# Batches 0 and 1 of an attention and MLP kernel: from pairs of heads with keys in chunks of 112 to quads of heads with keys in chunks of 64

## The chip, the core and the metric

The kernel runs on one core of a Trainium2 chip. The metric is the device time of one execution in microseconds, taken as the median over several runs. TensorE (PE), VectorE (DVE), ScalarE (ACT), GpSimd (POOL) and the sync engine (SP) each work through their own queue of instructions in order and wait for each other with semaphores.

## The reference

```python
def _attn_ref(q, k, v):            # 8 batches, 12 heads, 448 tokens, 64 per head
    scale = 1.0 / np.sqrt(q.shape[-1])
    scores = scale * np.matmul(q, k.transpose(0, 1, 3, 2))
    m = np.max(scores, axis=-1, keepdims=True)
    e = np.exp(scores - m)
    attn = e / (np.sum(e, axis=-1, keepdims=True) + np.exp(-m) + 1e-09)
    return np.matmul(attn, v)

def _moe_ref(x, w_in, w_out):      # x: 3584 x 768, w_in: 768 x 2048, w_out: 2048 x 768
    h = x @ w_in
    r = np.maximum(h, 0.0)
    return (r * r) @ w_out
```

The twelve heads of a token, side by side, are the row x of the second part. All inputs and the output are float32 in HBM. Since e is divided by its sum plus exp(-m), the maximum cancels, and the kernel computes exp(scores) / (sum + 1) without it.

## The kernel before

All matrix work is in float16. An order written out by hand sets what each engine does when; there is no scheduler behind it. Batch by batch, the attention of one batch is interleaved with the projections of the batches before it, so that TensorE always has something to stream.

**Attention.** Scores are computed transposed, keys on partitions and queries in columns. Queries and keys are first "flipped" on TensorE (transposed against an identity into PSUM, lines L191 and L211, then copied to the tile `qk`, L193 and L217). `exp` (L222) goes from the PSUM tile `sp`, of which there are two buffers, to the tile `et`. Row sums come from a matmul against a block of ones, which spreads the sum over 64 partitions; Ln with a bias and Exp with scale -1 on ACT turn it into the reciprocal `rcp` (L290 and L291, in quads L378 and L379). The values are a matmul of v against `et` (L273, in quads L390), and one multiplication on VectorE (L299, L302, L396) writes the normalised result to `xt`, the input of the projections.

**Two ways to tile it.** Batches 2 to 7 work in quads of four heads with keys in chunks of 64 (`visit`, L332 and L346; `values_quad`; `sums_quad`): a score or value matmul uses a 64x64 quarter of the array, and four run side by side. A quad is seven chunks, and one exponential covers 128 partitions by 896 elements. Batches 0 and 1 work in pairs of two heads with keys in chunks of 112 (P), four chunks for a pair: a score matmul uses 64 rows by 112 columns of the array (L241), a value matmul 112 rows by 64 columns (L273), and two run side by side. VectorE adds the exponentials of the four chunks first (`add_chunks`: L257 and L260 in batch 0, L253 and L255 in batch 1), so that the row sums are one matmul a head (L287).

**Stages.** Batch 0's queries come in two parts, the first 192 (FIRST) and then 256, each for six pairs; `units` lists them. While the first part runs TensorE has no projection work; `keep_warm` puts matmuls on zeros in between. From then on `tile_in` (L419: x times w_in, then ReLU and square on VectorE, L431 and L433, into `gs`) is handed out in pieces by `drain`, whose shares are written out for each unit. `tiles_in_early` starts two such tiles with the pairs that are ready. In mode COLS2 a projection matmul uses 128 rows by 64 columns of the array, two side by side. Batch 1 follows in six units of all 448 queries, with the rest of batch 0's input projection, and with the flips of batch 2's first two quads. Its last pair is finished inside the loop of batch 2.

From there a loop over the batches begins. `between` issues twelve or eleven visits of quads, with output projection tiles (`tile_out`, L491 in mode SQUARE, 64x64 quarters of the array) and values between them by a count of planned time; then eight input projection tiles run (`run(ins, ...)`), a second `between`, and eight more. `second` hands out the output tiles, in the order first and second half of the 768 columns; each half needs the matching half of `wout`.

**Loads.** q and k of the first three pairs come as float32 on the queues of SP and ACT (L119), one transfer of 224 KB each, into buffers of the exponentials' pool, and are cast by `cast` (L201 on ACT, L203 on VectorE). All else comes by GpSimd's queue, cast to float16 on the way, in this order: v, q and k of the other pairs (L108, L126), `win` in eight pieces (L132) with batch 1's first q and k in their middle, the rest of batch 1, then batch 2's q and k (L99) and `wout` (L136), which are issued after the last unit of batch 0, then batch 2's last quad, its v (L91) and the staged copies for batch 3 (L155). A load into a buffer that is in use waits, and holds up what GpSimd has queued behind it.

Of the kernel before, what the change touches and what calls it, by code (L numbers as in the profile page):

```python
# [16 lines left out]
def kernel(  # L17
# [9 lines left out]
    nc = tc.nc  # L27
# [4 lines left out]
    NPAIR = H // 2  # L32
# [3 lines left out]
    P = S // RUN  # L36
    NQ = H // 4
    KC = S // 64
    PAIRED = (0, 1)
# [15 lines left out]
    e_pool = ctx.enter_context(tc.tile_pool(name="e", bufs=4))  # L55
# [17 lines left out]
    q_r = q.rearrange("b h (p t) d -> b p h t d", t=RUN)  # L73
    k_r = k.rearrange("b h (p t) d -> b p h t d", t=RUN)
    v_r = v.rearrange("b h (p t) d -> b p h t d", t=RUN)
# [3 lines left out]
    whole, vns, qks, xts, naturals, stages = {}, {}, {}, {}, {}, {}  # L79
# [5 lines left out]
    def load_v_quads(b):  # L85
        vn = vns[b] = v_pool.tile([128, NQ, 2, KC, D], FP16, name="vn")
        for i in range(2):
            rows_ = vn[64 * i:64 * i + 64].rearrange("p g j c d -> p (g j) (c d)")
            parts = ((0, KC),) if b in ON_PE else ((0, KC - 1), (KC - 1, KC))
            for c0, c1 in parts:  # L90
                nc.gpsimd.dma_start(out=rows_[:, :, c0 * D:c1 * D], in_=quads_of(v, 64 * c0, 64, c1 - c0)[b, i])  # L91

    def load_natural_quads(b, g0, g1):
        t = nat.tile([128, RUN * 2 * S], FP16, name=f"nn{0 if g0 == 0 else 1}")
        w = 2 * S
        for n, r in enumerate((q, k)):
            part = t[:, n * (g1 - g0) * w:(n + 1) * (g1 - g0) * w].rearrange("p (h x) -> p h x", x=S)
            for i in range(2):
                nc.gpsimd.dma_start(out=part[64 * i:64 * i + 64], in_=quads_of(r, 0, 64, KC)[b, i][:, 2 * g0:2 * g1])  # L99
            for g in range(g0, g1):  # L100
                naturals["qk"[n], b, "quad", g] = part[:, 2 * (g - g0):2 * (g - g0) + 2].rearrange(
                    "p j (c d) -> p j c d", d=D)

    def load_v(b, p0, p1):
        hs = slice(2 * p0, 2 * p1)
        if b not in vns:
            vns[b] = v_pool.tile([P, H, RUN, D], FP16, name="vn")
        nc.gpsimd.dma_start(out=vns[b][:, hs], in_=v_r[b, :, hs])  # L108

    def load_natural(b, p0, p1):  # L110

        raw = b == 0 and p1 <= 3
        for n, r in (("q", q_r), ("k", k_r)):
            src = r[b, :, 2 * p0:2 * p1]
            if raw:
                if p0 == 0:
                    whole[n] = e_pool.tile([P, RUN * S], FP32, name="et")
                t = whole[n][:, p0 * 512:(p0 + 1) * 512].rearrange("p (h t d) -> p h t d", h=2, t=RUN)
                (nc.sync if n == "q" else nc.scalar).dma_start(out=t, in_=src)  # L119
            else:  # L120
                if p0 % 3 == 0 and n == "q":
                    whole["both"] = nat.tile([P, RUN * 2 * S], FP16, name=f"nn{p0 // 3}")
                w = NPAIR * RUN * D
                t = whole["both"][:, w * (n == "k"):w * (n == "k") + w].rearrange("p (h t d) -> p h t d", t=RUN, d=D)
                t = t[:, 2 * (p0 % 3):2 * (p0 % 3 + p1 - p0)]
                nc.gpsimd.dma_start(out=t, in_=src)  # L126
            for pr in range(p0, p1):
                naturals[n, b, pr] = t[:, 2 * (pr - p0):2 * (pr - p0) + 2]
# [55 lines left out]
    def transposes_quad(b, g):  # L184
        if b not in qks:
            qks[b] = qk_pool.tile([128, 3, COLS], FP16, name="qk")
        for n in range(2):
            tp = mp_tile(FP16).rearrange("p a x -> p (a x)")
            for c in range(KC):
                for j in range(2):  # L190
                    nc.tensor.transpose(tp[64 * j:64 * j + 64, 128 * c:128 * c + 128],  # L191
                                        naturals["qk"[n], b, "quad", g][:, j, c, :], ident)
            nc.vector.tensor_copy(  # L193
                qks[b][:, n, 2 * S * g:2 * S * (g + 1)].rearrange("p (i c x) -> p c i x", i=2, c=KC),
                tp[:, 0:2 * S].rearrange("p (c i x) -> p c i x", c=KC, i=2))

    def cast(b, pr):
        for name in "qk":
            f = flat.tile([P, 2, RUN, D], FP16, name=f"flat{name}")
            if pr < 2 and name == "k":  # L200
                nc.scalar.activation(out=f, in_=naturals[name, b, pr], func=AF.Copy)  # L201
            else:
                nc.vector.tensor_copy(f, naturals[name, b, pr])  # L203
            naturals[name, b, pr] = f

    def transposes(b, pr):
        tp = mp_tile(FP16)
        for i, name in enumerate("qk"):
            for s in range(RUN):
                for h in range(2):  # L210
                    nc.tensor.transpose(tp[64 * h:64 * h + 64, i, P * s:P * s + P],  # L211
                                        naturals[name, b, pr][:, h, s, :], ident[0:P, 0:P])
# [641 lines left out]
```

## Time and profile before

| | us |
|---|---|
| median of 3 runs | 407.98 (407.74 to 408.20) |
| the profiled execution | 407.64 |
| its span | 405.9 |
| TensorE busy | 394.9 (97%) |
| VectorE busy | 277.2 (68%) |
| ScalarE busy | 224.1 (55%) |
| GpSimd busy | 59.5 (15%) |
| L222, all exponentials to `et`, 132 instructions | 118.0 |
| L419, all input projection matmuls to `mp`, 1248 instructions | 109.0 |
| moved by DMA | 45.83 MB |

The profile is of one execution. Its span goes from the first to the last instruction on the core; the time of the execution has 1.7 us around it. Busy time of an engine counts each moment once, but the busy times of groups on TensorE overlap, since several matmuls run side by side, and can't be added. A timeline line gives start, length, engine, line of the kernel, operation, the tile written, the tiles read, the shape and the count; in brackets stands the time that the engine was idle before it and what ended the wait. PE is matmul and PEld the load of its stationary operand.

### The profile page before, as it was taken

The page shows a single profiled execution, that of the slowest core. Times are in us where ns is not written, and L with a number is a line of the kernel's source. Part 1 is how long each engine was busy: PE and PEld are TensorE (multiplying, and loading weights), DVE is VectorE, ACT ScalarE, POOL GpSimd, SP SyncE. Part 2 cuts the span into 40 slices and gives each one's busy share as a digit, 9 for nine tenths or more (in the row PEclk, how much of TensorE's full clock was granted, in tenths as well). Part 3 has the DMA queues.
Part 4 walks back from the last instruction along what each step waited for, and adds up shares of the span by engine and source line. Part 5 has one row for each costly group of instructions (what it writes and reads, how often), then busy time and mean ns, then how long its engine had stood idle before and what let it go on. Part 6 is the DMA issues. An engine that isn't in the chain of part 4 may idle for free.

```text
span 405.9 us, 14479 instructions
## 1 busy us (share of the span) xinstructions
PE 394.9 (97%) x6627; PEld 262.4 (65%) x6627; DVE 277.2 (68%) x507; ACT 224.1 (55%) x277; POOL 59.5 (15%) x93
## 2 busy tenths in 40 slices
PE   7899998999999999999999999999999999999997
PEld 3567676667676666757666675757666675555664
DVE  3778888786967867686967867686967868186000
ACT  4898986928465564836466473836466473100111
POOL 6524140005000320003200440005000000000000
PEclk9999999999999999999999999999999999999999
DMA  9999999498706794186925694186501020100222
GB/s 186 197 197 198 203 204 208 105 196 113 175 3 126 122 186 102 42 134 144 189 69 129 119 191 95 42 155 122 120 3 40 3 80 4 48 31 0 79 78 79
DMA packets 77118, 45.83 MB, mean 113 GB/s; under 512 B 46720, under 2 KB 71552, under 8 KB 77056
## 3 DMA queue, kind: packets, MB, share of 16 engines
q0 software_dynamic: 30128, 22.16, 36.5%
q1 hardware_dynamic: 46208, 22.05, 24.5%
q8 instruction: 52, 0.85, 0.9%
q10 hardware_dynamic: 720, 0.69, 0.7%
q14 instruction: 10, 0.08, 0.1%
HBM read 45.69 MB, written 17.93 MB: 157 GB/s over the span
## 4 chain that ended last, share of the span: by engine, by line
PE 87%; DVE 5%; ACT 3%; DMA 2%; issue 1%; ACTq 0%; DVEq 0%
PE mp L491 26%; PE mp L419 22%; PE mp L421 10%; PE xp L419 6%; PE mp L390 6%; PE sp L346 5%; PE xp L421 4%; ACT et L222 2%; DMA et<-in_k_dram 2%; PE sp L241 2%; PE xp L273 2%; PE sp L332 1%; PE mp L211 1%; PE xp L491 1%; PE sp L375 1%
## 5 line engine op out<-in xcount | busy, mean ns | idle before, releaser
L222 ACT ACTIVATE et<-sp 128x896 f16<-128x896 f32 (+3 forms) x132 | 118.0, 915 | 26.0 <-PE sp L346 13.0
L491 PE MATMUL mp<-wout,gs 64*64 64x384 f16 x1760 | 125.6, 323 | 0.0
L419 PEld LDWEIGHTS <-win 128*64 128x64 f16 x1536 | 85.0, 110 | 47.7 <-issue 7.2
L419 PE MATMUL mp<-xt,win 128*64 128x448 f16 (+2 forms) x1248 | 109.0, 324 | 2.2 <-DVE qk L193 1.3
L491 PEld LDWEIGHTS <-gs 64*64 64x64 f16 x2624 | 76.2, 107 | 23.0 <-issue 0.6
L491 PE MATMUL xp<-wout,gs 64*64 64x384 f16 x864 | 84.7, 323 | 0.0
L431 DVE TENSOR_SCALAR rt<-mp 128x448 f16<-128x448 f32 (+2 forms) x82 | 51.0, 622 | 19.0 <-PE mp L419 8.4
L433 DVE TENSOR_TENSOR gs<-rt 128x448 f16<-128x448 f16 (+2 forms) x128 | 50.4, 395 | 12.0 <-ACT rt L429 7.9
L222 ACT ACTIVATE nn<-sp 128x896 f16<-128x896 f32 x42 | 37.6, 913 | 14.0 <-PE sp L346 12.3
L429 ACT ACTIVATE rt<-mp 128x448 f16<-128x448 f32 x18 | 9.8, 543 | 60.0 <-PE mp L419 48.3
L498 DVE TENSOR_SCALAR ot<-mp 128x384 f32<-128x384 f32 x41 | 22.7, 554 | 27.3 <-PE xp L491 19.9
L181 POOL COPY flatq<-qk 64x384 f16<-64x384 f16 x20 | 13.6, 704 | 186.9 <-DMA qk<-stage_k 186.6
L421 PEld LDWEIGHTS <-gs 128*128 128x128 f16 x256 | 24.4, 98 | 15.1 <-issue 0.4
L346 PE MATMUL sp<-qk 64*64 64x224 f16 x720 | 32.9, 258 | 0.0
L419 PE MATMUL xp<-xt,win 128*64 128x448 f16 x288 | 31.3, 352 | 0.0
L421 PE MATMUL mp<-wout,gs 128*128 128x384 f16 (+2 forms) x192 | 29.6, 313 | 0.0
L346 PEld LDWEIGHTS <-qk 64*64 64x64 f16 x720 | 22.4, 119 | 10.7 <-issue 3.6
L500 ACT ACTIVATE ot<-mp 128x384 f32<-128x384 f32 (+2 forms) x12 | 5.6, 463 | 42.4 <-PE mp L421 42.4
L396 DVE TENSOR_TENSOR xt<-mp,rcp 128x448 f16<-128x448 f32 x34 | 19.7, 619 | 8.2 <-PE mp L390 7.8
L378 ACT ACTIVATE rcp<-sp,one_b 128x896 f32<-128x896 f32 x18 | 18.1, 1003 | 6.3 <-PE sp L371 6.3
L390 PEld LDWEIGHTS <-vn 64*64 64x64 f16 x504 | 14.4, 107 | 6.1 <-issue 0.4
L390 PE MATMUL mp<-et,vn 64*64 64x448 f16 x308 | 18.3, 349 | 0.0
(82 smaller groups left out, 392.6 us busy)
## 6 DMA issues: line engine op xcount, KB each, us to landing
out_dram<-ot SPq DMA_DIRECT2D x9, 384.0 KB, 2.3
win<-in_moe_w_in_dram POOLq DMA_DIRECT2D x8, 384.0 KB, 14.0
wout<-in_moe_w_out_dram POOLq DMA_DIRECT2D x4, 768.0 KB, 17.8
vn<-in_v_dram POOLq DMA_DIRECT2D x10, 288.0 KB, 5.4
out_dram<-ot SPq DMA_DIRECT2D x15, 192.0 KB, 3.0
stage_q<-in_q_dram POOLq DMA_DIRECT2D x4, 676.0 KB, 9.8
stage_k<-in_k_dram POOLq DMA_DIRECT2D x4, 676.0 KB, 12.3
out_dram<-ot SPq DMA_DIRECT2D x7, 288.0 KB, 6.0
```

What stands on the lines that cost most here:

```text
L181: nc.gpsimd.tensor_copy(km[rows_].rearrange("p h (x o) -> p h x o", o=2)[:, :, :, odd], src[:, :, S // 2 - 32:S // 2])
L222: nc.scalar.activation(out=out_, in_=in_, func=AF.Exp, scale=scale)
L346: nc.tensor.matmul(sp[64 * i:64 * i + 64, o, j * n:(j + 1) * n], keys, qk[r, 0, h * n:(h + 1) * n], start=True, stop=True)
L378: nc.scalar.activation(out=rcp, in_=zp[:, :, 0:S], func=AF.Ln, bias=one_b)
L390: nc.tensor.matmul(xps[i][64 * j:64 * j + 64, 0:S], vns[b][r, g, j, c, :], of_column(e[r], m, j), start=(c == 0), stop=(c == KC - 1))
L396: nc.vector.tensor_mul(xts[b][:, NQ * i + g, :], xps[i][:, 0:S], zqs[m][:, i, :])
L419: nc.tensor.matmul(out_[x:x + 64], lhsT[:, x:x + 64], rhs, start=start, stop=stop)
L421: nc.tensor.matmul(out_, lhsT, rhs, start=start, stop=stop)
L431: nc.vector.tensor_scalar(out=rt[:, 0:m], in0=hp[:, 0:m], scalar1=0.0, scalar2=None, op0=ALU.max)
L433: nc.vector.tensor_mul(gs[:, f0:f0 + per, t0 % RING:t0 % RING + n], r, r)
L491: nc.tensor.matmul(o[y:y + 64, 0:w], g[x:x + 64, y:y + 64], wout[x:x + 64, fb, n0:n0 + w], start=(fb == 0), stop=(fb == NFFB - 1))
L498: nc.vector.tensor_scalar(out=ot[:, n0:n0 + w], in0=op[:, 0:w], scalar1=OUT_SCALE, scalar2=None, op0=ALU.mult)
```

## The change

Batches 0 and 1 take the form of the others. The code of the pairs goes (`scores`, `add_chunks`, `values`, `row_sums`, `normalise`, `tiles_in_early`, `drain` and the list of units), and with it `keep_warm` but for the nine matmuls at the very start. Batch 0 keeps its two parts of 192 and 256 queries. Each part has three quads, and each quad four visits: two chunks of 64 keys in one exponential, and one chunk in the last. Its sums are no longer added on VectorE: all seven chunks accumulate on TensorE (`part_sums`), in a buffer of the scores' pool. Batch 1 uses `visit` and `values_quad`; VectorE adds six of its chunks to two, and `sums_quad` accumulates these two and the seventh chunk on TensorE. Sums and values of a quad are issued among the visits of the next one, and those of batch 1's last quad inside the loop of batch 2. Projection tiles are issued whole (`fill`) at written-out places. Inside a projection tile the order of the heads is such that the last quad comes last.

The first loads come by quad and by chunk: queries 0 to 2 (chunks of 64) and keys 0 to 2 of quad 0, keys 3 to 6, then queries 0 to 2 and all keys of quad 1; what is left of the queries of batch 0 comes later in one piece by GpSimd. `wout` is loaded in two halves, the second behind batch 2's last quad and v. The exponentials' pool has five buffers instead of four. Flips and their copies to `qk` are issued in pieces that follow the loads, and two pieces may share one PSUM tile. Batches 0 and 1 are stored in rows of seven tokens instead of four.

```diff
-    e_pool = ctx.enter_context(tc.tile_pool(name="e", bufs=4))
+    e_pool = ctx.enter_context(tc.tile_pool(name="e", bufs=5))
...
+    def transposes(b, g, *groups):
+        if b not in qks:
+            qks[b] = qk_pool.tile([128, 3, COLS], FP16, name="qk")
+        for pieces in groups:
+            tp = mp_tile(FP16).rearrange("p a x -> p (a x)")
+            o = 0
+            for n, c0, c1, copy in pieces:
+                flips(tp, o, b, g, n, c0, c1)
+                flipped(copy, tp, o, b, g, n, c0, c1)
+                o += 128 * (c1 - c0)
...
+    def part_visit(p, g, v):
+        q0, n = ((0, FIRST), (FIRST, S - FIRST))[p]
+        e = part_e(p, g)
+        cs = range(2 * v, min(2 * v + 2, KC))
+        sp = s_psum.tile([128, 2, 512], FP32, name="sp")
+        for c in cs:
+            for i in range(2):
+                for j in range(2):
+                    r = slice(64 * j, 64 * j + 64)
+                    x = (2 * g + i) * S
+                    o = (c - cs[0]) * n
+                    nc.tensor.matmul(sp[64 * i:64 * i + 64, j, o:o + n], qks[0][r, 1, x + 64 * c:x + 64 * c + 64],
+                                     qks[0][r, 0, x + q0:x + q0 + n], start=True, stop=True)
+        exp(e[:, cs[0]:cs[-1] + 1].rearrange("p c j n -> p j c n"),
+            sp[:, :, 0:len(cs) * n].rearrange("p j (c n) -> p j c n", n=n))
+
+    def part_sums(p, g):
+        n = (FIRST, S - FIRST)[p]
+        e = part_e(p, g)
+        zp = s_psum.tile([128, 2, 512], FP32, name="sp")
+        for c in range(KC):
+            for i in range(2):
+                for j in range(2):
+                    r = slice(64 * i, 64 * i + 64)
+                    nc.tensor.matmul(zp[64 * j:64 * j + 64, i, 0:n], ones[r], e[r, c, j], start=(c == 0),
+                                     stop=(c == KC - 1))
+        parts[p, g, "z"] = reciprocals(zp, n)
...
     def sums_quad(m, in_cols):
-        es = esq.pop(m)[:, 0:2 * S]
+        es = esq.pop(m)
+        sums = [es[:, 0:2 * S]]
+        if QUADS[m][0] == 1:
+            sums += [es[:, 2 * S:4 * S], chunk_quad(m, KC - 1)]
...
-    for pr in range(3):
-        load_natural(0, pr, pr + 1)
+    for g in range(2):
+        raw = e_pool.tile([128, RUN * S], FP32, name="et")
+        load_chunks(nc.sync, heads(raw, 0, 2, 3), 0, 0, g, g + 1, 0, 3)
+        if g == 0:
+            load_chunks(nc.scalar, heads(raw, 384, 2, 3), 1, 0, g, g + 1, 0, 3)
+            load_chunks(nc.sync, heads(raw, 768, 2, 4), 1, 0, g, g + 1, 3, KC)
+        else:
+            load_chunks(nc.scalar, heads(raw, 384, 2, KC), 1, 0, g, g + 1, 0, KC)
...
     keep_warm(9)
-    cast(0, 0)
-    transposes(0, 0)
-    keep_warm(1)
-    cast(0, 1)
...
+    cast(0, (0, 0, 3, nc.vector), (1, 0, 3, nc.scalar), (1, 3, KC, nc.vector))
+    transposes(0, 0, [(0, 0, 3, on_dve), (1, 0, 3, on_act)])
+    part_visit(0, 0, 0)
+    transposes(0, 0, [(1, 3, KC, on_dve)])
+    part_visit(0, 0, 1)
+    cast(1, (0, 0, 3, nc.vector), (1, 0, KC, nc.vector))
+    transposes(0, 1, [(0, 0, 3, on_dve), (1, 0, 3, on_dve)], [(1, 3, KC, on_dve)])
+    part_visit(0, 0, 2)
+    part_visit(0, 0, 3)
+
+    def part(p, g, prev, before_second, before_third, before_last):
+        part_visit(p, g, 0)
+        if prev:
+            part_sums(*prev)
+        part_visit(p, g, 1)
+        before_second()
+        part_visit(p, g, 2)
+        if prev:
+            part_values(*prev)
+        before_third()
+        part_visit(p, g, 3)
+        before_last()
...
+    part(1, 0, (0, 2), lambda: rest_of_q(1), lambda: rest_of_q(2), lambda: (queue(0, FIRST), fill()))
+    part(1, 1, (1, 0), fill, none, fill)
+    part(1, 2, (1, 1), fill, lambda: transposes_quad(1, 0), fill)
...
+    full_quad(0, lambda: part_sums(1, 2), lambda: (part_values(1, 2), queue(FIRST, S - FIRST)),
+              {1: fill, 3: lambda: transposes_quad(1, 1), 4: fill, 5: fill})
+    load_natural(2, 0, 2)
+    load_half(0)
+    full_quad(1, lambda: sums_quad(0, False), lambda: values_now(0),
+              {1: fill, 3: lambda: transposes_quad(1, 2), 4: fill, 5: fill})
+    load_natural(2, 2, 3)
+    load_v(2)
+    load_half(HALF)
+    stage(3)
+    full_quad(2, lambda: sums_quad(1, False), lambda: values_now(1),
+              {1: fill, 3: fill, 4: lambda: transposes_quad(2, 0), 5: fill, 6: lambda: transposes_quad(2, 1)})
+    fill(len(ins))
```

In the calls of `transposes` and `cast`, 0 and 1 stand for queries and keys, followed by the first chunk and the one behind the last; `on_dve` and `on_act` name the engine of the copy. `full_quad` issues the seven visits of a quad with the sums and values of the quad before it behind visits 0 and 2, and then what the last argument lists by chunk.

## The prediction

> **What bounds the kernel now.** I read the slices first, then windows cut at the places where TensorE's work changes its kind, then the timeline at those places, then the groups kept apart by shape.
>
> ```profile
> span 405.9 us, 14479 instructions
> PE 394.9 (97%) x6627; PEld 262.4 (65%) x6627; DVE 277.2 (68%) x507; ACT 224.1 (55%) x277; POOL 59.5 (15%) x93
> PEclk9999999999999999999999999999999999999999
> DMA  9999999498706794186925694186501020100222
> ```
>
> TensorE is busy for 97% of the span at a full granted clock, so a change gains only where TensorE gets less to stream or waits less. The transfer engines are full for the first seven slices (71 us).
>
> ```profile
> 5.40:21.70 16.30, 14.25 (x222) 8.84 (x222) 10.97 (x26) 13.43 (x20) 8.76 (x11) 1.00 1.41 204
> 21.70:46.00 24.30, 23.09 (x402) 17.23 (x398) 19.48 (x40) 22.48 (x29) 8.48 (x11) 1.00 1.42 199
> 46.00:68.60 22.60, 20.86 (x339) 15.40 (x335) 19.87 (x37) 18.06 (x24) 4.90 (x8) 1.00 1.29 205
> 68.60:81.60 13.00, 12.35 (x280) 8.44 (x279) 9.41 (x15) 12.09 (x15) 0.00 (x0) 1.00 0.60 127
> ```
>
> The columns are length, then PE, PEld, DVE, ACT and POOL busy, clock, DMA share, GB/s. The four stretches are: attention of batch 0 without projection work; the stage with all tiles of `tile_in` for batch 0; its second half; the first `between` of batch 2. ACT is nearly full in the first (13.43 of 16.3). Behind 81.6 us both kernels issue the same work in the same order, on a TensorE that is 97% to 100% busy, so what the change does to 81.6 us is what it does to the time.
>
> ```profile
> 4.83 0.56 DVE L203 CAST flatq<-et 112x512 f16<-112x512 f32 x1 [3.10 <-DMA et<-in_q_dram]
> 7.00 0.63 ACT L201 ACTIVATE flatk<-et 112x512 f16<-112x512 f32 x1 [1.21 <-DMA et<-in_k_dram]
> 7.54 2.94 ACT L222 ACTIVATE et<-sp 112x768 f16<-112x768 f32 x4
> 21.78 1.51 PE L419 MATMUL mp<-xt,win 128*64 128x192 f16 x32
> 24.57 0.43 PE L241 MATMUL sp<-qk 64*112 64x256 f16 x4
> 24.93 0.60 PE L419 MATMUL mp<-xt,win 128*64 128x192 f16 x10
> 66.42 2.24 PE L419 MATMUL mp<-xt,win 128*64 128x256 f16 x38
> 68.59 0.38 PE L332 MATMUL sp<-qk 64*64 64x448 f16 x4
> 81.60 1.65 PE L419 MATMUL mp<-xt,win 128*64 128x448 f16 x12 [0.64 <-ACT rcp L290]
> ```
>
> The marks are: first exponential 7.54 us, first projection 21.78, first quad of batch 2 68.59, projection of batch 1 81.60. A change of tile shape costs TensorE about 0.15 us: four matmuls of 256 columns, two side by side, stream in 4x256/2/2.4 = 213 ns, yet the next group starts 360 ns later; 38 of 256 columns stream in 2.03 us and L332 starts 2.17 us later. (2.4 columns a ns is the pace of long runs, such as the 38 matmuls.)
>
> ```profile
> L222 ACT ACTIVATE et<-sp 112x896 f16<-112x896 f32 x24 | 20.6, 913 | 4.5 <-PE sp L241 4.3
> L222 ACT ACTIVATE et<-sp 112x1024 f16<-112x1024 f32 x12 | 11.7, 1020 | 1.2 <-PE sp L241 1.2
> L222 ACT ACTIVATE et<-sp 112x768 f16<-112x768 f32 x12 | 9.4, 804 | 1.2 <-PE sp L241 0.9
> L378 ACT ACTIVATE rcp<-sp,one_b 128x896 f32<-128x896 f32 x18 | 18.1, 1003 | 6.3 <-PE sp L371 6.3
> L379 ACT ACTIVATE rcp<-rcp 128x896 f32<-128x896 f32 x18 | 17.1, 950 | 0.6
> ```
>
> An exponential costs about 0.16 us plus 0.84 ns an element of a partition, whatever the partitions; a 384 column one then 0.48, a 512 one 0.59.
>
> **ScalarE and VectorE get lighter.** Exponentials of batch 0: nine of 768 and three of 384, nine of 1024 and three of 512, 8.7 + 10.9 = 19.6 us by these rows, for 12x0.804 + 12x1.020 = 21.9. Batch 1: 21 of 896 for 24, 19.2 for 21.9 us. VectorE loses the adds of batch 0 (24 instructions at L257 and L260, 12.0 us) and trades 18 adds of batch 1 (11.1 us) for six of 1792 elements (about 1.1 each, 6.6 us). I count VectorE at nothing: it is 68% busy and its adds made TensorE wait 0.4 us in all; that cover is gone only where it is on a chain, which is the start, below.
>
> **TensorE streams the same.** Chunks of 64 keys fill the array four ways: per batch 21 rounds of 448 columns for scores and 21 for values instead of 24 and 24, so six rounds of 187 ns less, 1.1 us a batch. The sums take it back: 21 rounds in batch 0 for 6 (+2.8 us), 9 for 6 in batch 1 (+0.6). Five warm-up groups leave (six matmuls of 512 columns, 1.3 us). Over both batches: -2.2 + 3.4 - 1.3, about zero. So the question is where TensorE waits.
>
> **The start, 3.2 us later.** Loads: SP issues six and ACT four transfers at about 0.45 us each where both issued three; bytes are equal (1.31 MB against 1.38), so the first pieces land at about 4.9 and 5.2 as now, and the second transfers on SP, keys 3 to 6 of quad 0, about where the second pair lands now (7.0). The order of VectorE's queue is new: cast of queries, cast of keys 3 to 6, then the copy of the flipped queries. That copy waits behind a cast that waits for DMA. The flips of the keys write the tile that it reads, and wait for it. Chain: 7.0 landed, 0.45 cast, 0.35 copy, 0.4 six flips with their tail, 0.5 copy on ACT, 0.35 scores, and five handovers of 0.05: first exponential at 9.3 instead of 7.54. The same pattern follows for quad 1: flips of keys 3 to 6 and their copy let the second exponential start at 10.3; then VectorE casts queries (0.4) and 896 columns of keys (0.7), copies, and TensorE, which has the flips of quad 1 ahead of the third visit, gets to that visit at 12.05. Third exponential: 12.4. ACT then has ten exponentials of batch 0's first part (seven of 768, three of 384: 7.1), three pairs of Ln and Exp of 384 columns (0.577 + 0.522 each, 3.3) and two exponentials of 1024 (2.0) before the scores that stand ahead of the first `fill`: 12.4 us, nearly without gaps, since scores run two buffers ahead. First projection at 24.9 to 25.0, against 21.8. From below: keys land at 6.5 and VectorE's casts take what the fastest rows take, 2.2 us; from above: ACT has a gap of 0.3 a part, 4.2. I take 3.2.
>
> **From the first projection to batch 2, 2.4 us shorter.** Streaming left at 25.0: 16 projection tiles (8x0.96 + 8x1.28 = 17.9), scores 5.4, sums 3.4, values 4.85, five quads of flips (28 in a group of 1.00 us at L191, some 0.2 of it tail: 3.9): 35.4. Before, from 21.8: 36.4 in 46.8 us, of which 43 changes of tile shape are 6 and waits 4.4. Now the changes: 4 and 6 in the two parts left, 9, 8 and 9 in the quads, 36 in all, 5.4 us. Waits by walking TensorE and ACT in order: 0.3 a part where the second visit waits for the first exponential behind the sums, 1.0 at each of two changes of quad (the sums take the score buffer of chunk 6 and wait for its exponential, then the second visit waits again): 3.0. Ends: 0.5 if the lighter ACT is always ahead, 4.4 if waits stay as they were. I take 3.4, nearer the walk. 35.4 + 5.4 + 3.4 = 44.2: batch 2 at 69.2 against 68.6.
>
> **The first `between`, 0.45 longer.** It takes over sums and values of batch 1's last quad (3 and 7 rounds, 1.9 us) for those of the last pair (0.93 us), and ACT gets a second Ln and Exp. Visit 11 waits for eleven exponentials of 0.917 and one pair of 1.95: 12.4 us with the first scores; flips and two changes of shape 1.05. 13.45 against 13.0, in which the 0.64 wait at L419 is gone.
>
> **Transfers.** Behind the first loads they are the same bytes in smaller pieces. GpSimd's issue of batch 2's first quads now waits for the flips of quad 1 of batch 1 (about 43 us by the walk); 7.9 MB ahead of it are through at 41 us at 200 GB/s, so the queue stands idle some 4 us with its start-up. The first half of `wout` lands near 57 us, the second, behind quad 2 and v, at 71; they are needed at 69.2 and about 5.4 later. Nothing to pay, with 3 us in hand. Stores of batches 0 and 1 stay two to a tile; nothing waits for them.
>
> Sum: +3.2 - 2.6 + 0.45 = +1.05 us, with 46.8 - 44.2 = 2.6. The profiled execution is 407.64 (span 405.9 and 1.7 around it), 0.3 under the median of 407.98; on the median 409.0.
>
> **The clock without warm-up.** In the rows, the nine first matmuls of 512 columns take 3.59 us, 0.40 each and half the later pace; afterwards no window shows under 1.00. The new chain leaves TensorE idle from about 5.6 to 7.9 us and little used to 12. If it went slow until the first projection, a part's 2.4 us of streaming would be 4.9 against ACT's 4.0: 0.9 for each of three parts and 1.0 of flips and scores on the chain, +3.7. The Trainium skill, in "TensorE: Matmul & The Clock Gate", Part 1, says that the clock falls to half after an idle window of about 3.4 us. By that the gap of 2.3 us alone would not trip it, and the price would be nothing; no row here shows a gap of such a length.
>
> **Rivals.**
> *Faster*: waits nearly vanish, since ACT has 36 us of work for 44 us of TensorE: 35.4 + 5.4 + 0.5, -5.5 instead of -2.6, and the start costs 2.7: -2.35, 405.6. For: the unmatched 8 us. Against: waits at sums come from the score buffers' order, not from ACT's load.
> *Cold clock*: +3.7, 412.7. Decides if a window between 6 and 12 us shows a clock under 1.00.
> *Late weights*: transfers slower by 5 us or held longer; the second output tile then waits about 2.5: 411.5. Against: the 3 us in hand.
> *Nothing to see*: the start's loss and the stage's gain cancel, 408.0; an end of my own case.
>
> **Numbers.** Forecast's mechanism 0.52 (407.2 to 411.0), faster 0.25, cold clock 0.13, late weights 0.10. 0.2%, 0.8 us, is what a measurement can tell. Below 407.2: 0.22 of the faster case. Within 0.8: 0.03 of it and 0.23 of the forecast's, 0.26. Above: 0.52. The range 405.6 to 412.2 leaves out the outer part of both ends.
>
> **Signs.** Right: first exponential near 9.3, first projection tile near 25, batch 2's first visit near 69, two pairs of Ln and Exp among its first twelve exponentials. Wrong: a first exponential at 7.5 to 8, a projection of batch 1 before 81, a wait on `wout` or a clock under 1.00.

## The result and the profile after

| | before | after |
|---|---|---|
| median | 408.09 us (407.74 to 408.23, 4 runs) | 418.43 us (417.50 to 420.12, 4 runs) |
| profiled execution, span | 407.64, 405.9 | 420.12, 418.3 |
| first exponential | 7.54 | 13.36 |
| first projection | 21.78 | 33.02 |
| batch 2's first visit | 68.59 | 80.50 |
| projection of batch 1 | 81.60 | 94.20 |
| from there to the end of the span | 324.3 | 324.1 |

The ratio is 1.0259, 95% interval 1.0220 to 1.0299: 10.3 us slower, where 1.05 were predicted and 412.2 was the end of the range. The profiled execution is the slowest of its four, 1.7 us above the median; what stands below of single waits is of that execution. (The kernel before, timed again beside the experiments, had medians between 407.8 and 408.6.)

The page of the kernel after. Its loss begins in the first three slices of 10.5 us, where TensorE's row reads 4, 6 and 7 tenths:

```profile
span 418.3 us, 15167 instructions
...
PE 396.6 (95%) x6981; PEld 265.5 (63%) x6981; DVE 264.1 (63%) x479; ACT 219.1 (52%) x268; POOL 63.0 (15%) x102
...
PE   4678888999999999999999999999999999999996
...
PEclk9999999999999999999999999999999999999999
```

The same row of the kernel before, in slices of 10.1 us:

```profile
PE   7899998999999999999999999999999999999997
```

The timeline of the start of the kernel after (start, length, engine, line, shape, in brackets the idle time before and what ended it):

```profile
7.53 0.36 DVE L520 CAST half<-et 128x384 f16<-128x384 f32 x1 [5.79 <-DMA et<-in_q_dram]
...
7.94 0.53 PE L168 MATMUL mp<-ident,half 128*64 128x128 f16 x6 [2.73 <-DVE half L520]
...
10.74 0.62 DVE L520 CAST half<-et 128x512 f16<-128x512 f32 x1 [2.85 <-DMA et<-in_k_dram]
11.28 0.34 DVE L171 COPY qk<-mp 128x384 f16<-128x384 f16 x1
11.67 0.53 PE L168 MATMUL mp<-ident,half 128*64 128x128 f16 x6 [3.20 <-DVE qk L171]
...
13.36 0.81 ACT L190 ACTIVATE et<-sp 128x768 f16<-128x768 f32 x1 [0.64 <-PE sp L224]
```

The chain is the predicted one, link for link: the cast of keys 3 to 6 waits for its transfer, the copy of the flipped queries stands behind it, and the key flips wait for the copy (3.20 us). But the keys were there at 10.7, not 7.0. In the trace's packets GpSimd's queue moves its first bytes at 2.9 us (before: 7.0). By 7 us the queues of SP and ACT have started 0.80 MB (before: 1.22) and GpSimd's 0.24 (before: almost none), and SP and ACT are served in full at 11.9 instead of 8.4 us. SP's issues of the small transfers also take longer, 0.61 to 0.82 us each against 0.40 to 0.46.

The same view, later:

```profile
18.40 1.33 PE L238 MATMUL sp<-et,ones 64*64 64x192 f16 x28
...
24.27 0.77 PE L238 MATMUL sp<-et,ones 64*64 64x192 f16 x28 [0.28 <-ACT et L190]
...
30.14 0.57 PE L251 MATMUL mp<-et,vn 64*64 64x192 f16 x17
...
32.08 0.44 PE L251 MATMUL mp<-et,vn 64*64 64x192 f16 x11 [1.36 <-issue]
...
33.02 1.18 PE L368 MATMUL mp<-xt,win 128*64 128x192 f16 x24
...
44.19 0.29 PE L251 MATMUL mp<-et,vn 64*64 64x256 f16 x1 [0.97 <-issue]
...
57.29 0.57 PE L329 MATMUL sp<-half,ones 64*64 64x448 f16 x8 [1.55 <-DVE half L312]
...
68.14 0.57 PE L329 MATMUL sp<-half,ones 64*64 64x448 f16 x8 [1.75 <-DVE half L312]
...
80.50 0.38 PE L286 MATMUL sp<-qk 64*64 64x448 f16 x4
...
94.20 1.11 PE L368 MATMUL mp<-xt,win 128*64 128x448 f16 x10
```

Three things stand here. The same 28 sums take 1.33 us at 18.40 and 0.77 at 24.27: TensorE runs at half pace until about 24 us, though the clock row above reads full. Twice a group of 28 value matmuls stops in its middle for no wait that the profile knows ("issue"), 1.36 and 0.97 us; a group of scores has such a stop of 0.49 us at 25.3. And the sums of batch 1's quads wait 1.55 and 1.75 us for VectorE's second add.

### The profile page after: what moved, and what is told of

It reads as the page before. It is cut to its first block, busy times and chain, and to the rows that moved or that the text cites. A ratio compares the mean times of both kernels' runs of the same rounds, so it can differ in the third digit from the quotient of the medians.

```text
span 418.3 us, 15167 instructions
## 1 busy us (share of the span) xinstructions
PE 396.6 (95%) x6981; PEld 265.5 (63%) x6981; DVE 264.1 (63%) x479; ACT 219.1 (52%) x268; POOL 63.0 (15%) x102
## 4 chain that ended last, share of the span: by engine, by line
PE 90%; DVE 3%; ACT 3%; DMA 2%; issue 1%; SPq 1%; DVEq 0%
PE mp L425 24%; PE mp L368 23%; PE mp L370 10%; PE xp L368 8%; PE mp L342 6%; PE sp L300 5%; PE xp L370 4%; PE sp L286 2%; PE mp L168 2%; ACT et L190 2%; DMA et<-in_k_dram 2%; PE sp L329 2%; PE sp L224 2%; PE xp L425 1%; PE mp L251 1%
## 5 line engine op out<-in xcount | busy, mean ns | idle before, releaser
L190 ACT ACTIVATE et<-sp 128x896 f16<-128x896 f32 (+4 forms) x129 | 114.0, 898 | 36.8 <-PE sp L300 13.0
L368 PEld LDWEIGHTS <-win 128*64 128x64 f16 x1536 | 82.7, 110 | 47.6 <-issue 6.1
L368 PE MATMUL mp<-xt,win 128*64 128x448 f16 (+2 forms) x1152 | 101.9, 330 | 0.0
L425 PEld LDWEIGHTS <-gs 64*64 64x64 f16 x2624 | 77.2, 107 | 22.2 <-issue 0.5
L380 DVE TENSOR_SCALAR rt<-mp 128x448 f16<-128x448 f32 (+2 forms) x78 | 48.5, 621 | 25.6 <-PE mp L368 15.0
L382 DVE TENSOR_TENSOR gs<-rt 128x448 f16<-128x448 f16 (+2 forms) x128 | 50.6, 395 | 11.9 <-ACT rt L378 7.9
L368 PE MATMUL xp<-xt,win 128*64 128x448 f16 (+2 forms) x384 | 36.9, 331 | 0.0
L370 PE MATMUL mp<-wout,gs 128*128 128x384 f16 (+2 forms) x192 | 29.6, 313 | 0.0
L199 ACT ACTIVATE rcp<-sp,one_b 128x896 f32<-128x896 f32 (+2 forms) x27 | 24.9, 921 | 8.6 <-PE sp L329 8.1
L300 PEld LDWEIGHTS <-qk 64*64 64x64 f16 x720 | 22.3, 119 | 10.7 <-issue 3.6
L346 DVE TENSOR_TENSOR xt<-mp,rcp 128x448 f16<-128x448 f32 x37 | 21.6, 619 | 8.9 <-PE mp L342 7.6
L200 ACT ACTIVATE rcp<-rcp 128x896 f32<-128x896 f32 (+2 forms) x27 | 23.4, 867 | 0.9
L342 PE MATMUL mp<-et,vn 64*64 64x448 f16 x350 | 23.0, 349 | 0.0
```

The lines of the kernel that those rows point to most:

```text
L190: nc.scalar.activation(out=out_, in_=in_, func=AF.Exp, scale=scale)
L199: nc.scalar.activation(out=rcp[:, :, 0:n], in_=zp[:, :, 0:n], func=AF.Ln, bias=one_b)
L200: nc.scalar.activation(out=rcp[:, :, 0:n], in_=rcp[:, :, 0:n], func=AF.Exp, scale=-1.0)
L300: nc.tensor.matmul(sp[64 * i:64 * i + 64, o, j * n:(j + 1) * n], keys, qk[r, 0, h * n:(h + 1) * n], start=True, stop=True)
L342: nc.tensor.matmul(xps[i][64 * j:64 * j + 64, 0:S], vns[b][r, g, j, c, :], of_column(e[r], m, j), start=(c == 0), stop=(c == KC - 1))
L346: nc.vector.tensor_mul(xt_of(b)[:, NQ * i + g, :], xps[i][:, 0:S], zqs[m][:, i, :])
```

## The experiments

**The clock.** First the kernel before, without the six later matmuls of `keep_warm` (the nine at the very start stay):

```diff
-    keep_warm(1)
...
-            keep_warm(1)
...
-        if i in (1, 3, 5):
-            keep_warm(1 + i // 5)
```

> The kernel before without its six warm-up matmuls of the first 18 us, nothing else changed. Theory A: they hold the clock; without them some flips and scores between 6 and 20 us run at half pace and the time rises by 0.5 to 3 us. Rival: TensorE is busy often enough there with its own work, the pace stays, and the time falls by up to 0.5 us or stays.

Measured: 412.07 us (10 runs), ratio 1.0066 (1.0027 to 1.0105), so 1.1 to 4.3 us. First projection 24.5 instead of 21.8, projection of batch 1 85.4 instead of 81.6. Windows of this run (length, busy us of PE, PEld, DVE, ACT and POOL with counts, clock, DMA share, GB/s):

```profile
9.00:10.00 1.00, 0.52 (x17) 0.37 (x16) 0.48 (x3) 1.00 (x2) 0.25 (x1) 1.00 1.43 190
...
10.50:11.00 0.50, 0.50 (x16) 0.28 (x10) 0.47 (x2) 0.50 (x1) 0.50 (x2) 0.94 1.45 198
11.00:11.50 0.50, 0.50 (x8) 0.27 (x4) 0.47 (x2) 0.23 (x1) 0.50 (x2) 0.50 1.46 194
...
27.50:28.00 0.50, 0.50 (x8) 0.21 (x6) 0.00 (x0) 0.12 (x1) 0.00 (x0) 0.50 1.49 192
28.00:28.50 0.50, 0.50 (x14) 0.50 (x10) 0.00 (x0) 0.50 (x1) 0.00 (x0) 0.99 1.46 199
```

Here the clock column does show it: full until 10.94, half from there to 28.0. TensorE had no long gap before that: no wait shown between 5 and 11 us was over 0.5. It was busy for 0.52 of the one microsecond shown from 9.00, and for 2.31 of the whole 3.41 ahead of the fall. Without those six matmuls the kernel before falls to half pace as well, and loses 2.7 us by the ratio.

Then the kernel after with 36 such matmuls more (the expectation says 33): 19 at the start for nine, 14 and 3 between the query and key flips of quads 0 and 1, and two or three ahead of each further step, the last two behind the fourth visit.

```diff
                 flipped(copy, tp, o, b, g, n, c0, c1)
                 o += 128 * (c1 - c0)
+                if b == 0 and g < 2 and n == 0 and c0 == 0:
+                    keep_warm((14, 3)[g])
...
-    keep_warm(9)
+    keep_warm(19)
```

> The changed kernel with 33 matmuls on zeros put back into the gaps of the start (10 more ahead of the flips of quad 0, 14 between its query and key flips, the rest in twos and threes up to the fourth visit), nothing else. Theory A, the clock: in the changed kernel's trace the sums of quad 0 at 18.4 us take 1.33 us and those of quad 1 at 24.3 take 0.77, so TensorE runs at half pace from about 8 to 24 us, and the granted clock in the profile's rows does not show it. With the gaps filled the first sums take about 0.8 us, the first projection starts 2.5 to 4 us earlier than 33.0, and the time falls by as much, to about 415. Rival, loads only: the first exponential and the first projection stay within 0.5 us of 13.4 and 33.0, the time stays at 418, since the start waits for keys 3 to 6 and then for ScalarE.

Measured: 418.21 (417.04 to 420.0), ratio 1.0247 (1.0207 to 1.0287), no different from the change. Its timeline:

```profile
12.02 0.81 ACT L192 ACTIVATE et<-sp 128x768 f16<-128x768 f32 x1 [0.46 <-PE sp L226]
...
17.11 0.75 PE L240 MATMUL sp<-et,ones 64*64 64x192 f16 x28
...
28.89 1.18 PE L370 MATMUL mp<-xt,win 128*64 128x192 f16 x24
```

The sums of quad 0 now take 0.75 us. From first exponential to first projection there are 16.9 us instead of 19.7, 2.8 less. But 1.36 of that is the stop at 30.7 us of the change, which has no counterpart here ahead of the first projection, so at most 1.4 is left for the pace. The projection of batch 1 comes at 90.8, 3.4 earlier than in the profile of the change, but the median is only 0.2 lower: behind 90.8 this execution takes 1.1 longer (325.2 for 324.1), and of the 2.3 that are left (417.8 for 420.12) 1.7 are what the change's profiled execution lies above its median, and 0.4 what this one lies below. The stage behind the first projection takes 48.2 us instead of 47.5; two stops of 0.86 and 0.85 us stand in it. So the half pace is real, but the median shows no gain from ending it alone.

**The loads.** GpSimd's first load is held until keys 3 to 6 have landed, by one small copy on GpSimd that reads them:

```diff
+    make_identity(nc, ident)
+    hold = consts.tile([128, 1], FP32)
+    nc.gpsimd.tensor_copy(hold, raw0[:, 768:769])
     load_v(0, 0, 1)
-    make_identity(nc, ident)
```

> The changed kernel with one thing moved: GpSimd copies one column of keys 3 to 6 of quad 0 before it issues its first load, so none of its loads shares the transfer engines with the loads of SP and ACT until those keys have landed. Theory B, contention: GpSimd's v packets start at 2.7 us in the changed kernel and at 7.0 in the kernel before, and take engine time from q and k; held back, keys 3 to 6 land at 7.5 to 8.5 instead of 10.7 and the first exponential starts at 10 to 11 instead of 13.4; the time falls by 2 to 3 us unless the loads of quad 2 then come late. Rival C, issue: SP needs 0.6 to 0.8 us for each of its transfers, and the keys are third and fourth in its queue, behind 1792 byte packets of ScalarE's queue; then they land not before 9.5 and the time gains under 1 us or loses.

Measured: keys 3 to 6 cast at 8.08 instead of 10.74, first exponential 10.5, first projection 29.8. The queues of SP and ACT are through at 7.9 instead of 11.9 us. So GpSimd's early packets were what delayed the keys; in all five profiles with the loads of the change this cast starts between 9.94 and 10.80. The time did not follow: 419.84 (418.45 to 422.21), ratio 1.0289 (1.0242 to 1.0336). GpSimd's queue has moved nothing by 10 us, 0.45 MB in the change, and its loads feed quad 2, but no wait of TensorE for them stands in this trace. The sums of quad 0 are still at half pace (1.34 us). What took the gain back is not shown.

The cast of keys 3 to 6 is moved behind the first visit, so that VectorE's copy of the queries does not stand behind it:

```diff
-    cast(0, (0, 0, 3, nc.vector), (1, 0, 3, nc.scalar), (1, 3, KC, nc.vector))
+    cast(0, (0, 0, 3, nc.vector), (1, 0, 3, nc.scalar))
     transposes(0, 0, [(0, 0, 3, on_dve), (1, 0, 3, on_act)])
     part_visit(0, 0, 0)
+    cast(0, (1, 3, KC, nc.vector))
```

> The changed kernel with the cast of keys 3 to 6 on VectorE moved behind the first visit, so that the copy of the flipped queries does not wait for it. Theory D, the order of VectorE's queue that the prediction priced: queries land at 7.5, the copy is done at about 8.3, the first exponential starts at about 9.8 instead of 13.4; the second then still waits for the keys at about 12.5. So ScalarE gains one exponential of 0.8 us: the first projection comes about 0.8 to 1.2 earlier, the time falls by about 1 us. Rival, that the whole delay of the first exponential counts: 3 us or more.

Measured: first exponential at 9.82, 3.5 earlier; the second, which needs keys 3 to 6, at 12.49; first projection 31.0; time 418.07 (417.22 to 418.3), ratio 1.0236 (1.0209 to 1.0263). The order of the queue set the first exponential, as predicted. The time is 0.4 us under the change's, inside the spread of either; that the chain to the first projection goes through the later pieces is argued from the second exponential.

Both together, with 16 warm-up matmuls:

> The changed kernel with the three edits of the start together: GpSimd's loads held until keys 3 to 6 have landed, the cast of these keys behind the first visit, and 16 small matmuls on zeros in the gaps (4 more ahead of the first flips, the rest in twos and threes). If load contention, the order of VectorE's queue and the clock are separate causes, each real, they add: first exponential at about 8 us instead of 13.4, the sums of quad 0 in 0.8 us instead of 1.3, first projection at 24 to 25.5 instead of 33.0, and the time falls by 7 to 8 us, to about 411. Rival, ScalarE or instruction supply set the first projection: it stays behind 28 and the time above 414.

Measured: 420.74 (418.87 to 426.35), ratio 1.0292 (1.0250 to 1.0334): no gain. Its profile is of an execution far above the others, and I read nothing from it. So three edits that each moved their own mark bought nothing together, and no run shows why.

**The sums.** VectorE adds chunks 0 to 2 to chunks 3 to 5 of each part, so that TensorE accumulates four totals instead of seven chunks:

```diff
+        nc.vector.tensor_add(added_of[p, g], e[:, 0:3], e[:, 3:6])
...
+        totals = [added[:, c] for c in range(3)] + [e[:, KC - 1]]
...
-        for c in range(KC):
+        for c, total in enumerate(totals):
```

> The changed kernel with one part of the change taken half back: batch 0's chunks 0 to 2 and 3 to 5 are added on VectorE (one instruction a quad part), and TensorE accumulates four totals instead of seven. 72 matmuls leave TensorE's program. Theory E, instruction supply: TensorE stops for 0.7, 1.6 and 1.2 us in the middle of groups of 28 small matmuls, just behind refills of its instructions; fewer instructions make these stops shorter or fewer, and with 1.7 us less to stream the time falls by 2 to 4 us. Rival F, streaming alone: 1 to 1.7 us. Rival G, the adds put the sums behind VectorE: no gain or a loss of up to 2 us.

Measured: 418.45 (418.2 to 418.65), ratio 1.0251 (1.0231 to 1.0271). The stops in the middle of groups are gone (no wait of that kind over 0.5 us), and from first projection to batch 2 there are 46.0 us, not 47.5. Yet the time is that of the change. That the start took it back is argued, not shown: three of its four executions have a mean clock of 0.975 to 0.978, where three of the change have 0.984. Its profile also shows that the clock row of the change misleads. A window of it, and the flips of quad 1's queries in its timeline:

```profile
14.00:18.00 4.00, 2.73 (x42) 1.84 (x41) 2.40 (x6) 1.81 (x3) 2.58 (x5) 0.50 1.45 196
```

```profile
15.82 0.53 PE L168 MATMUL xp<-ident,half 128*64 128x128 f16 x6 [0.45 <-DVE qk L171]
```

In the change the same six flips take the same 0.53 us at 15.69, with 1.00 in the column; at full pace they take 0.36. The records behind the column say why: in the trace of the change they begin only at 23.98 us, where the full pace returns (in the kernel before at 4.22), and the page draws time without a record as full. The other three executions of the change have a mean clock of 0.984, which is 0.016 x 415.8 = 6.7 us of clock lost, 13 us at half.

**VectorE's second add** of batch 1's quads is issued behind visit 5 instead of visit 6:

```diff
+            if c == 5:
+                add_quad(g, 1)
...
-        add_quad(g, 1)
```

> The changed kernel with the second add of each quad of batch 1 issued behind visit 5 instead of behind visit 6, ahead of a ReLU and square in VectorE's queue. Theory H: in the changed kernel the sums of quads 0 and 1 wait 1.7 and 1.9 us for that add, which stands behind the ReLU of the projection tile of visit 5; now they wait only for the last exponential, about 0.8 us less each, and the time falls by 1.3 to 2 us. Rival: the wait for the score buffer takes its place, under 0.5 us.

Measured: 418.07 (417.56 to 420.74), ratio 1.0260 (1.0216 to 1.0304), no different from the change. The wait at the sums changes its owner, and shrinks from 1.75 to 0.83 us:

```profile
65.72 0.57 PE L329 MATMUL sp<-half,ones 64*64 64x448 f16 x8 [0.83 <-ACT et L190]
```

The two waits shrink by 1.6 us together, which the median does not show. What is left ends with an exponential; that it is the score buffer that the sums take, the 1.0 that the prediction had put there, is argued from the order. The start of this kernel is that of the change, and its trace has the clock's records: half from 7.53 to 21.18 us.

```profile
PEclk8599999999999999999999999999999999999999
```

**All of it.** Held loads, order, light warm-up, four totals and the earlier add:

> The three together: the start of the fifth run, the sums of the sixth, the adds of the seventh. If the causes are separate the gains add: 7.5, 2.5 and 1.5 us, about 407, level with the kernel before or below it. If the start only moves waits into the stage with the projection tiles, above 411.

Measured: 415.29 (414.45 to 416.39), ratio 1.0175 (1.0147 to 1.0204): the first clear gain, 3.1 us on the change. First exponential 8.3, first projection 29.9, projection of batch 1 89.2. TensorE waits 1.07 and 1.49 us for the queries of quad 2, which the hold delays, and inside the second of these waits (20.31 to 21.80) the half pace comes back, from 20.97 to 31.2 us by the clock column. TensorE had been busy for 1.75 of the 3.41 us ahead.

The next run shortens the hold to the first queries and leaves the sums as in the change; the one after adds the four totals and 14 more warm-up matmuls (its expectation says 12):

> The changed kernel with GpSimd's first load held only until the first queries of quad 0 have landed (not until keys 3 to 6 have), the cast of keys 3 to 6 behind the first visit, some ten warm-up matmuls more, and the second add of batch 1's quads issued behind visit 5; sums as in the change. If the late loads of quad 2 were what gave the start's gain back in the kernel with all edits, this hold starts GpSimd some 2 us earlier, the first exponential stays at 8.3 to 9.5, the first projection comes at 28 us or earlier and the time is 413 to 415. If TensorE's half pace between 20 and 30 us is what holds the start, the first projection stays at 29 to 30 us and the time at 415.5 to 418, since the sums are seven rounds again.

> As the run before, but the sums of batch 0 from VectorE's adds (four rounds on TensorE for seven) and 12 more warm-up matmuls between the flips of the queries and of the keys of quad 0 and at the very start. If the half pace is decided by how long TensorE stands still before 12 us, the sums of quad 0 run at full pace, the first projection comes at 27 us or earlier and the time is 411 to 413.5. If the half pace returns whatever fills those gaps, because TensorE has too little work until the projections begin, the first projection stays at 29 to 30 us and the time at 414.5 to 416.

Measured: 416.05 (ratio 1.0202, 1.0180 to 1.0224) and 413.88 (1.0144, 1.0124 to 1.0164), both with a clock of 0.996 to 1.000 in every execution. First projection at 27.3 and 28.9, batch 2's first visit at 75.2 and 75.0, projection of batch 1 at 88.9 and 88.7. The second one's later start (its warm-ups sit ahead of the key flips, first exponential 11.3 against 8.6) is made up by a shorter stage, 46.1 against 47.8 us. So full pace throughout did not bring the first projection to 27 us or earlier in the second one. In the first one, with a full clock, the stops ("issue") stand alone:

```profile
26.06 0.27 PE L253 MATMUL xp<-et,vn 64*64 64x192 f16 x1 [1.85 <-issue]
...
27.34 1.18 PE L370 MATMUL mp<-xt,win 128*64 128x192 f16 x24
```

**Batch 1 alone.** The kernel before with its batch 0, loads and warm-up untouched, and batch 1 in quads (chunks added in full on VectorE, sums one round of four matmuls):

```diff
-    PAIRED = (0, 1)
+    PAIRED = (0,)
...
-    QUADS = [(b, g) for b in range(2, B) for g in range(NQ)]
+    QUADS = [(b, g) for b in range(1, B) for g in range(NQ)]
...
+    full_quad(0, last_unit_sums, last_unit_values,
+              {1: (fill,), 3: (lambda: transposes_quad(1, 1),), 4: (fill,), 5: (fill,), 6: (fill,)})
...
+    full_quad(1, lambda: sums_quad(0, False), lambda: values_now(0),
+              {0: (fill,), 1: (fill,), 4: (lambda: transposes_quad(1, 2), fill), 5: (fill,)})
```

> Batch 1 alone in quads: batch 0 keeps its pairs, loads and warm-up matmuls of the kernel before. If the loss of the change is all in the start (late keys, cold TensorE), the first exponential stays at 7.5 and the first projection at 21.8 us, as in the kernel before, and the time is that of the kernel before or less: batch 1's quads save six rounds of 448 columns and ScalarE 2.7 us of exponentials, so 405 to 408. If quads of 64 keys cost by themselves in this stage (waits of the sums for VectorE's adds, 1.75 and 1.95 us in the changed kernel, and stops of TensorE's instruction supply), batch 2's first visit comes at 70 or later instead of 68.6 us and the time is 409 to 411.

Measured: 408.27 (12 runs), ratio 1.0009 (0.9998 to 1.0021). First projection 21.0, batch 2's first output tile 66.4 instead of 68.8, but the projection of batch 1 at 83.4 instead of 81.6. What the stage gained went back to one wait, here in the timeline, and to the pace: the clock column reads 0.50 from 70.62 to 74.04 us, 1.7 us of clock lost, behind 3.41 us in which TensorE was busy for 0.88.

```profile
70.22 0.38 PE L375 MATMUL sp<-half,ones 64*64 64x448 f16 x4 [2.53 <-DVE half L362]
```

Six of the 12 executions have that loss in their mean clock (0.995 or 0.996) and take 408.56 to 409.10; the six at 1.000 take 407.47 to 407.98.

The last run takes that wait away: these sums behind the fourth visit of batch 2 instead of the second, two output tiles ahead of the values that follow instead of one, and values directly behind the sums of a quad.

```diff
-            if c == (2 if g == 0 else 3):
+            if c == 2:
                 prev_values()
...
-            extras[1] = [m - 1]
+            extras[3] = [m - 1]
...
+        ahead = 2 * (b == 2)
```

> Batch 1 alone in quads, with two waits of that run taken away: sums of batch 1's last quad behind the fourth visit of batch 2 instead of the second (there TensorE waited 2.53 us for VectorE's last add, L362), two output tiles ahead of its values instead of one; and the values of a quad directly behind its sums, so that the wait of the next visit for its score buffer (0.83 us at 49.90 and 60.77) lies beside 28 value matmuls. If these waits were what kept batch 1's quads from paying, the projection of batch 1 comes 2.5 to 4 us earlier, at 79.5 to 81 us, and the time is 404 to 406, under both kernels. If VectorE's queue is the bound there and the wait only moves to the next sums, the time stays at 407.5 to 408.5.

```profile
70.74 0.38 PE L375 MATMUL sp<-half,ones 64*64 64x448 f16 x4 [0.36 <-DVE half L362]
...
82.10 1.11 PE L419 MATMUL mp<-xt,win 128*64 128x448 f16 x10
```

Measured: 406.98 (12 runs, 406.59 to 407.41), ratio 0.9965 (0.9946 to 0.9983): 1.2 us under the kernel before on the medians, with an interval clear of 1, and between the two expectations. The mean clock is 0.999 or 1.000 in all 12, so part of what it gains on the run before is half pace that no longer comes. The wait is 0.36, yet the projection of batch 1 comes at 82.1, 1.3 earlier than in the run before and still 0.5 later than in the kernel before: TensorE waits at other places of that stretch instead (it is busy for 13.74 of the 15.4 us ahead of it). Behind 82.1 the profiled execution takes 323.4 us to the end, 0.9 less than the kernel before does. Of that 0.35 lies ahead of the next batch's input projection (22.23 us for 22.58), as in the change; the rest no run explains. So the gain on the kernel before shows only behind the stage that was edited, and that the quads of batch 1 make it is not shown.

So batch 1 in quads, with its adds made in full on VectorE, costs nothing. In the form that the change gives it, with three rounds of sums, it was not run alone, and the waits of 1.55 and 1.75 us stand there. By the marks 11.2 of the 12.6 us of the profiled execution are lost ahead of the first projection, on the side of batch 0: its loads, its quads and the warm-up that went with its pairs. These were not run apart (quads under the loads of the kernel before, or the new loads under pairs). With every mend tried, projections still start 5.5 to 8 us late (27.3 to 29.9), and some 6 us (413.88 against 407.77) have no cause that a run shows.

## Why the prediction was wrong, by its own steps

The sum up to the projection of batch 1 was +1.05 and is +12.60 in the profiled execution. The 11.55 between them by stage: first exponential 13.36 for 9.3, 4.06; from there to the first projection 19.66 for 15.7, 3.96; from there to batch 2 47.48 for 44.2, 3.28; first `between` 13.70 for 13.45, 0.25.

*The start: the landing of keys 3 to 6.* This term failed. I took 7.0 us, "about where the second pair lands now", from equal bytes on SP and ACT. Both halves of that were unsafe: the issue of a small transfer costs up to 0.82 us, and GpSimd's queue, which I had given no part in the first 7 us, shares the transfer engines from 2.9 us. The held load shows the second: 8.08 for 10.74, so 2.7 of the 3.7 that the term was short. The bounds let the data land early (6.5) and never late; the upper end, 4.2, only varied what ACT does. The rest of the chain (order of VectorE's queue, copy, flips, handovers) stood: 10.74 to 13.36 is 2.6 us, for 2.3 reckoned.

*The clock.* Its mechanism was in the list of rivals, with 0.13 and 3.7 us. It came; in the profiles it takes at most 1.4 of the 3.96 behind the first exponential (1.36 more are the stop at 30.7 us, and some 1.2 stay open), and the kernel before loses 1.1 to 4.3 us with it. The price of 3.7 is not confirmed, since the run that ends the half pace gains 0.2 on the median. The chance was wrong, and so was the sign that I named for it, a clock under 1.00, which the profiled execution does not show, for want of records, while its matmuls take longer, the sums 1.7 times as long. A duration of a known group is the safer reading. The Trainium skill, in "TensorE: Matmul & The Clock Gate", Part 1, gives about 3.4 us for the window over which TensorE's activity is judged. The runs agree on the length: half pace lasted 17.1 us in the kernel before without its warm-up, 10.2 with all edits, 20.5 in the run with the four totals (8.68 to 29.15), which are 5, 3 and 6 times 3.4. They do not agree with my reading that TensorE must stand idle for a whole window. In the run with the earlier add, whose start is that of the change, it fell at 7.53, within a gap of 2.84 us. In the kernel before without its warm-up it fell with no wait above 0.5 us, on a TensorE busy for 68% of the 3.41 us ahead.

*The instruction supply* was in no step. The 7 rounds of sums and the values are many short matmuls (28 loads and 28 matmuls in 0.6 to 0.8 us), and TensorE issues 212 and 206 such pairs in the 10 us from 30 and from 40 us, for 184 and 142 before. Each long stop lies during or just behind a read of 16 KB on the instruction queue (29.6, 41.9 us). I had counted the sums as streaming time (+2.8). The stops move with the reads: in the seven kernels whose sums of batch 0 are seven rounds, each of the 25 stops over 0.4 us of this kind between 6 and 60 us begins 0.5 to 2.0 us after the start of such a read. The three kernels with four totals, 72 matmuls fewer, and the four with batch 0 in pairs have such reads and none of these stops. That speaks for the cause; that it is the supply and not something else at these places was not isolated.

*The stage: waits.* 3.4 had been taken, from a walk, between 0.5 and 4.4. TensorE stands still for 5.25 us of this stage, above the upper end: 1.55 and 1.75 for VectorE's adds where 1.0 each was meant for the score buffer, 0.26 to 0.36 at each of the three visits behind the sums where 0.3 stood, and the stop of 0.97. That is 1.85 of the 3.28 that the stage was short; streaming and one more change of shape are about 0.25, and some 1.2 lie in TensorE's busy time and stay open. "I count VectorE at nothing" is the step that failed here: its cover is gone not only at the start but wherever an add of 1.1 us, issued behind the last visit, is the last thing that the next sums need. With the earlier add 0.83 a quad is left, near the walk's 1.0. The term of streaming was right: 35.5 for 35.4, with 37 changes of shape for 36.

*What held.* The first `between` grew by 0.70 for 0.45. Nothing waits for `wout`, so the late weights are not it, although GpSimd's queue stands idle from 43.3 to 54.0 us, longer than the 4 us reckoned. The second half of `wout` lands at 83.0 us where 71 was reckoned; it is not missed since the stage that needs it came 11 us later too, which is luck. ScalarE and VectorE did get lighter, by 5 and 13 us of busy time, and that bought nothing. The rival of a faster stage fell with the waits. The sign was right; the size was not.

## What to carry to other kernels

A kernel's first microseconds are a chain of landings, and a landing time from another layout is not a price: count which queues will share the transfer engines and what each issue costs, and let the range hold what the data may do. Small matmuls that only keep TensorE occupied between waits can be worth microseconds (here 1.1 to 4.3 in the kernel before); before one takes them out, one should look at how long a known group lasts behind the spot where they stood, not at the clock row alone. And of a change that does two things, try the halves: here batch 1 alone cost nothing, and with its waits moved the kernel was 0.35% faster, so the 10 us lie with the other half, which was not run alone.

## What was not expected of the hardware

- The clock row of one execution read 1.00 while TensorE ran at half pace for some 16 us (28 sums in 1.33 us for 0.77): its clock records begin at 23.98 us. Another kernel with the same matmul durations read 0.50.
- Half pace came in stretches of 3.4, 10.2, 13.7, 17.1 and 20.5 us, and came back under way: at 20.97 us, 0.7 into a gap of 1.5 us, on a TensorE busy for 51% of the 3.41 us ahead, and at 70.62 us behind a gap of 2.53.
- TensorE stopped for 0.97 to 1.85 us in the middle of a group of small matmuls for which the profile shows no wait, close behind reads of 16 KB on the instruction queue.
- GpSimd's first packets moved at 2.9 us where they had moved at 7.0, though its first issue is at 1.24 and 1.48 us in the two kernels. What decides that stays open.
